# A convolution feeding a multiplicative FFN: the first group's last two rounds convolved by VectorE and GpSimd

## The chip, the cores and the metric

One Trainium2 chip, one of its cores. The metric is the device time of one execution in microseconds (us). The engines of the core: TensorE (PE in the profile; PEld its weight loads), VectorE (DVE), ScalarE (ACT), GpSimd (POOL) and SyncE (SP). SyncE, ScalarE and GpSimd issue DMA transfers, each on a queue of its own. Every engine works through its instructions in the order in which the program lists them.

## The reference

```python
# x (8, 3904, 192), weight (8 heads, 7 taps)
w = softmax(weight, axis=-1)
x_pad = concatenate([zeros((8, 6, 192)), x], axis=1)       # each sequence
out[b, s, h, g] = sum_k w[h, k] * x_pad[b, s + k, h * 24 + g]
x = out.reshape(31232, 192)
a = x @ w1                                                # (192, 1024)
b = x @ w2                                                # (192, 1024)
h = a * b @ w3                                            # (a * b) @ w3, (1024, 1024)
return h @ w_out                                          # (1024, 192)
```

A causal convolution with 7 taps over the tokens of each sequence, the same taps for the 24 channels of a head, and then a network in which two products are multiplied elementwise. The inputs are float32; the kernel computes in bfloat16 with float32 sums. It uses (a * b) @ (w3 @ w_out), so that W = w3 @ w_out (1024 x 192) is made once.

## The kernel before

**Rows and rounds.** The 31,232 tokens are cut into two halves ("rows" r = 0 and 1) of TS = 15,616, which run side by side: one on partitions 0 to 63, the other on 64 to 127, since 192 channels are three chunks of 64. A round is CH = 512 tokens of both halves; there are 31 (the last is half as long). Four rounds make a group. For each group the kernel runs the first products of its four rounds (`first_product`: for each of eight tiles of 128 columns, a and b by 12 matmuls at line 489, a cast of a by ScalarE at 497, the multiplication by VectorE at 508), and then its second products (`second_product`, line 540, one call per round and half, eight per group), whose results ScalarE copies to `osb` (545) and a DMA stores (552). `xT`, the convolved tokens with the channels on partitions, is a ring of four rounds.

**Where the convolved tokens come from.** There are three ways.

- *Blocks* (`SIZES`): windows of 64 tokens of which 58 come out (`ST`). TensorE multiplies a window by a banded matrix of taps (`conv`, line 398), ScalarE or VectorE evicts (419). Blocks 0 to 4 are transposed by TensorE straight into `xT` (rounds 0 to 3 and a bit more); from block 5 on they go to a DRAM buffer `rows` (`store`), and DMA transposes on SyncE's queue (`transposes`, 471) bring them into `xT`.
- *Separate blocks* (`ALONE`): 18 windows, 1,024 tokens, for the first two rounds of a half group; group p convolves them while its second products run, with `load_alone` (342) before and `store_alone` after.
- *Shared rounds* (`SHARED`): two rounds of 512 tokens, laid out with 128 stretches of tokens on partitions. GpSimd computes heads 0 to 3 with multiplications and additions (`shared_head`, lines 325 to 334) and VectorE heads 4 to 7 (317, 320; ScalarE starts each at 315). `load_shared` (279) brings the tokens, `pad_shared` (292) writes zeros over the six tokens ahead of a sequence's start, where a stretch begins with one; `store_shared` (364) writes `rows`. The tap k = 6 is taken first and reads nothing of those zeros; the taps k = 5 and lower read them.

Before the change, group 0 had no shared part: its second products had blocks 5, 6 and 7 between them (20, 20 and 14 windows), which made rounds 4 to 9. Shared and separate parts began with group 1 (rounds 10 and 11 shared, 12 and 13 separate).

**Order.** It is written out by hand: the program text gives the order on every engine, and a tile with several buffers makes an instruction wait for the last user of its buffer (`xb` has five, `xw` two: W3 transposed and the shared tokens; `convo` two). GpSimd in the beginning issues the loads of x and of the weights and copies weights; then `store(4, ...)` and W_out's load `wo_b` (664), `pace` (665: a two-element copy that makes GpSimd wait until W3's transposes are nearly done), and the loads of blocks 5, 6 and 7. SyncE transposes W3 (569). W = w3 @ w_out is made by `w3_product` (575) after round 3. The taps for the shared rounds are normalized in `wv` (lines 688 to 697) around that.

Of the kernel before, what the change touches and what calls it, by code (L numbers as in the profile page):

```python
# [16 lines left out]
def kernel(  # L17
# [30 lines left out]
    LAST = S - (WB - 1) * ST  # L48
# [9 lines left out]
    NB = len(SIZES)  # L58
# [3 lines left out]
    MAXN = SIZES[GRID - 1]  # L62

    def tok(i):
        return (i // WB) * S + (i % WB) * ST
# [40 lines left out]
    xb_of, zero_rows = {}, {}  # L106
# [5 lines left out]
    def load_x(b, parts=(0, 1)):  # L112
        tiles = xb_of.setdefault(b, [])
        zeros_of = zero_rows.setdefault(b, [])
        for i0, n in [v for e, v in enumerate(halves_of(b)) if e in parts]:
            xb = work.tile([128, n, D], BF16, tag="xb", bufs=5, name="xb")
            w = 0
            while w < n:
                i = i0 + w
                m = min(n - w, WB - i % WB)  # L120
                at_end = i + m == NWIN
                if at_end:
                    m -= 1
                if m:
                    for r in range(NS):
                        nc.gpsimd.dma_start(out=xb[Q * r:Q * r + Q, w:w + m, :],  # L126
                                            in_=x_spans(r, i, m))
                if i % WB == 0:
                    zeros_of += [(xb, 0, w), (xb, 1, w)]
                w += m  # L130
                if at_end:
                    nc.gpsimd.memset(xb[Q:128, w, :], 0.0)
                    t = tok(NWIN - 1) - PAD
                    nc.gpsimd.dma_start(out=xb[0:Q, w, :], in_=x_rows[t:t + Q, :])
                    nc.gpsimd.dma_start(out=xb[Q:Q + PAD + LAST, w, :],
                                        in_=x_rows[TS + t:TS + t + PAD + LAST, :])
                    w += 1
# [18 lines left out]
    diag = const.tile([128, Q + PAD], BF16)  # L156
    nc.vector.memset(zeros, 0.0)
# [45 lines left out]
    for i in range(2):  # L203
        copy_w(1, i, nc.gpsimd.tensor_copy)
    load_w(3)
# [130 lines left out]
    def load_alone(p):  # L336
        b, n = GRID - 1 + p, NA // 2
# [9 lines left out]
    def store_alone(p):  # L347
        convo, n = convo_of[GRID - 1 + p], NA // 2
# [75 lines left out]
    def store(b, first=0, last=NWIN, queue=nc.sync):  # L424
        n = SIZES[b] // 2
        last = min(last, FIRST[b] + 2 * n)
        stored[0] = tok(last) if last < NWIN else TS
        convo = convo_of[b]
        for c in range(2):
            i0 = FIRST[b] + c * n  # L430
            w, end = max(0, first - i0), min(n, last - i0)
            while w < end:
                left = WB - 1 - (i0 + w) % WB
                m = min(end - w, max(1, left))
                src = convo[Q * c:Q * c + ST, w:w + m].rearrange("s w k r g -> s w (k r g)")
                j0 = tok(i0 + w)
                if left == 0:
                    queue.dma_start(out=rows[j0:j0 + LAST, :], in_=src[0:LAST, 0, :])
                else:
                    dst = rows[j0:j0 + ST * m, :].rearrange("(w s) c -> s w c", s=ST)  # L440
                    for s0, s1 in ((0, 48), (48, ST)):
                        queue.dma_start(out=dst[s0:s1], in_=src[s0:s1])  # L442
# [196 lines left out]
    load_w3(CH)  # L639
    w3_transposes(0, range(JT))  # L640
# [4 lines left out]
    def send(last):  # L645
# [3 lines left out]

    first_product(0, {  # L650
        4: seq([(conv, 2, 0, 4)]),
# [12 lines left out]
    nc.gpsimd.dma_start(out=wo_b, in_=wor)  # L664
    P(out=pace, in_=w3T[0:1, JT - 3, DFF - 2:DFF])
# [8 lines left out]
    def zero(b):  # L674
        for xb, r, w in zero_rows.pop(b, []):
            nc.gpsimd.memset(xb[Q * r:Q * r + PAD, w, :], 0.0)
# [12 lines left out]
    nc.vector.tensor_tensor(  # L689
        out=wv, in0=wv, in1=top.unsqueeze(2).to_broadcast([128, H, K]), op=ALU.subtract)  # L690
    w3_product(0)
    nc.scalar.activation(out=wv, in_=wv, func=ACT.Exp)
    nc.vector.reduce_sum(out=top, in_=wv, axis=AX.X)
    nc.vector.reciprocal(out=top, in_=top)
    nc.vector.tensor_tensor(
        out=wv, in0=wv, in1=top.unsqueeze(2).to_broadcast([128, H, K]), op=ALU.mult)
    for jt in range(1, JT):
        w3_product(jt)
# [22 lines left out]
    for p, rounds in enumerate(groups):  # L721
# [3 lines left out]
        if p in SHARED:  # L725
# [6 lines left out]
            if p + 1 in SHARED:  # L732
                pad_shared(p + 1)
# [47 lines left out]
```

## Time and profile before

| | |
|---|---|
| median of 3 runs | 516.44 us (516.05 to 517.52) |
| profiled execution | 515.89 us, of which 514.2 are its span |
| TensorE busy | 508.4 us |
| VectorE busy | 401.1 us |
| ScalarE busy | 353.1 us |
| GpSimd busy | 321.4 us |

The profile is that of one execution. Its page gives each engine's busy time, the span in 40 slices, the DMA queues, the chain of waits that ended last, and the costliest groups of instructions by line; other views list the chain, or one engine's instructions, in order of time. In a row of the timeline stand the start, the length, the engine, the line, what it writes from what, the count, and in brackets the idle time ahead of it with what ended it. In a row of a group: the count, the least, median and greatest length in nanoseconds, the first and last start. `L489` is line 489 of the code. Rounds 0 to 3 run from about 9 to 59 us, W is made until 64.4, and group 0's second products end at 88.88.

### The profile page before, as it was taken

What the parts mean: (1) busy time and instruction counts of PE and PEld (TensorE: products, weight loads), DVE (VectorE), ACT (ScalarE), POOL (GpSimd) and SP (SyncE); (2) the same over time, 40 slices, a digit from 0 to 9 for tenths busy, and PEclk for the clock granted to TensorE, in tenths of its full rate; (3) what the DMA queues carried; (4) which work ended last, traced back from release to release, by engine and by line L of the source; (5) the groups of instructions that cost most, each with busy time, mean ns of one, the idle gap of its engine ahead of it and who ended that gap; (6) DMA issues with size and microseconds to landing.
All of it is one profiled execution on the core that took longest, in us unless ns stands there. A gap on an engine that the chain in (4) does not pass through costs nothing.

```text
span 514.2 us, 13632 instructions
## 1 busy us (share of the span) xinstructions
PE 508.4 (99%) x5608; PEld 339.1 (66%) x5608; DVE 401.1 (78%) x471; ACT 353.1 (69%) x469; POOL 321.4 (63%) x447
## 2 busy tenths in 40 slices
PE   8999999999999999999999999999999999999997
PEld 4555798454894458945598445985459845498587
DVE  6778723899959999499994999949999499972970
ACT  6887645777657776577765777657776577744762
POOL 8601534299999999699984999749997491000000
PEclk9999999999999999999999999999999999999999
DMA  8989999992965992787728787288842851035004
GB/s 118 155 152 127 134 216 231 207 197 54 193 193 149 137 108 94 237 146 102 95 93 248 141 104 91 93 255 134 93 51 94 259 112 32 2 102 171 6 3 155
DMA packets 137410, 67.91 MB, mean 132 GB/s; under 512 B 98899, under 2 KB 135939, under 8 KB 137283
## 3 DMA queue, kind: packets, MB, share of 16 engines
q0 software_dynamic: 48096, 26.92, 36.4%
q1 hardware_dynamic: 89105, 40.01, 32.7%
q8 instruction: 44, 0.72, 0.6%
q14 instruction: 19, 0.16, 0.1%
q10 hardware_dynamic: 146, 0.10, 0.1%
HBM read 39.60 MB, written 36.56 MB: 148 GB/s over the span
## 4 chain that ended last, share of the span: by engine, by line
PE 96%; DVE 2%; ACT 1%; issue 0%; ACTq 0%; DVEq 0%
PE pairs L489 60%; PE pairs L540 32%; PE pairs L398 2%; DVE abT L508 1%; PE pairs L575 1%; ACT asb L497 1%; PE pairs L451 1%; PE pairs L213 1%; DVE cprod L254 0%; ACT convo L419 0%; DVE convo L584 0%; ACT xT L463 0%; PE pairs L263 0%; PE pairs L615 0%; ACT osb L545 0%
## 5 line engine op out<-in xcount | busy, mean ns | idle before, releaser
L508 DVE TENSOR_TENSOR abT<-asb,pairs 128x1024 bf16<-128x1024 bf16 (+1 forms) x245 | 298.2, 1217 | 69.5 <-ACT asb L497 53.0
L489 PE MATMUL pairs<-xT,wd 64*128 64x512 bf16 (+2 forms) x3000 | 319.8, 371 | 0.7 <-DVE abT L508 0.3
L497 ACT CAST asb<-pairs 128x1024 bf16<-128x1024 f32 (+1 forms) x245 | 247.1, 1009 | 67.7 <-PE pairs L489 67.4
L489 PEld LDWEIGHTS <-wd 64*128 64x128 bf16 x3000 | 160.7, 94 | 153.6 <-issue 1.5
L540 PE MATMUL pairs<-W_sb,abT 128*128 128x192 bf16 x1952 | 165.0, 246 | 0.0
L540 PEld LDWEIGHTS <-abT 128*128 128x128 bf16 x1952 | 159.9, 98 | 5.3 <-issue 5.1
L545 ACT COPY osb<-pairs 128x384 f32<-128x384 f32 x122 | 58.6, 480 | 83.4 <-PE pairs L540 82.6
L331 POOL TENSOR_TENSOR acc<-acc,term 128x384 f32<-128x384 f32 (+1 forms) x120 | 107.3, 894 | 9.4
L328 POOL TENSOR_TENSOR term<-xv,wv 128x384 f32<-128x384 bf16 (+1 forms) x144 | 107.7, 748 | 0.5 <-DMA xv<-zeros 0.5
L317 DVE SCALAR_TENSOR_TENSOR pairs<-xv,wv,pairs 128x384 f32<-128x384 bf16 (+1 forms) x120 | 68.7, 572 | 7.2 <-ACT pairs L315 3.4
L364 POOL DMA_DIRECT2D rows<-y x6 | 3.7, 614 | 70.2 <-DVE y L320 61.3
L334 POOL TENSOR_TENSOR y<-acc,term 128x192 bf16<-128x192 f32 (+5 forms) x60 | 26.5, 467 | 1.9
L419 ACT CAST convo<-pairs 128x864 bf16<-128x864 f32 (+9 forms) x49 | 26.5, 613 | 0.2
L325 POOL TENSOR_TENSOR acc<-xv,wv 128x384 f32<-128x384 bf16 (+1 forms) x24 | 18.3, 764 | 9.7 <-DMA xv<-in_x_dram 9.6
L419 DVE CAST convo<-pairs 128x960 bf16<-128x960 f32 (+4 forms) x10 | 8.2, 858 | 17.2 <-PE pairs L398 17.2
L320 DVE SCALAR_TENSOR_TENSOR y<-xv,wv,pairs 128x192 bf16<-128x192 bf16 (+5 forms) x60 | 18.0, 351 | 1.1
L126 POOL DMA_DIRECT2D xb<-in_x_dram x20 | 13.9, 715 | 4.1 <-DMA xb<-in_x_dram 2.3
L342 POOL DMA_DIRECT2D xb<-in_x_dram x20 | 15.1, 772 | 0.0
L552 POOL DMA_DIRECT2D out_dram<-osb x8 | 6.1, 763 | 12.3 <-ACT osb L545 9.3
L279 POOL DMA_DIRECT2D xv<-in_x_dram x12 | 13.0, 1087 | 0.0
L315 ACT ACTIVATE pairs<-xv,wv 128x384 f32<-128x384 bf16 (+1 forms) x24 | 12.8, 550 | 0.0
L442 POOL DMA_DIRECT2D rows<-convo x2 | 1.1, 544 | 18.1 <-ACT convo L419 18.1
(65 smaller groups left out, 86.9 us busy)
## 6 DMA issues: line engine op xcount, KB each, us to landing
out_dram<-osb SPq DMA_DIRECT2D x52, 384.0 KB
xv<-in_x_dram POOLq DMA_DIRECT2D x10, 672.0 KB, 9.7
xb<-in_x_dram POOLq DMA_DIRECT2D x20, 216.0 KB, 7.3
rows<-y POOLq DMA_DIRECT2D x5, 768.0 KB, 5.9
out_dram<-osb POOLq DMA_DIRECT2D x8, 384.0 KB, 5.2
w3rows<-in_moe_w_dram POOLq DMA_DIRECT2D x2, 1024.0 KB, 11.8
xb<-in_x_dram POOLq DMA_DIRECT2D x8, 240.0 KB, 8.0
rows<-convo SPq DMA_DIRECT2D x6, 288.0 KB
```

The source lines that it names most:

```text
L317: f.scalar_tensor_tensor(out=flat, in0=xs(k), scalar=tap(k), in1=flat, op0=ALU.mult, op1=ALU.add)
L320: f.scalar_tensor_tensor(out=dst, in0=xv[:, 0:W, r, h * G + cs.start:h * G + cs.stop], scalar=tap(0), in1=by_row[:, :, r, cs], op0=ALU.mul ...
L325: f.tensor_tensor(out=flat, in0=xs(PAD), in1=wide(PAD), op=ALU.mult)
L328: f.tensor_tensor(out=term.rearrange("p (m g) -> p m g", g=G), in0=xs(k), in1=wide(k), op=ALU.mult)
L331: f.tensor_tensor(out=acc, in0=acc, in1=term, op=ALU.add)
L334: f.tensor_tensor(out=dst, in0=by_row[:, :, r, cs], in1=term[:, :, r, cs], op=ALU.add)
L419: f[e % len(f)](out=dst, in_=part)
L489: nc.tensor.matmul(p[:, r, e * n:e * n + n], wd[i][rs, k, ft * 128:(ft + 1) * 128], xT[k][rs, r0 + c0:r0 + c1], start=(k == 0), stop=(k == ...
L497: nc.scalar.copy(out=asb, in_=pa)
L508: nc.vector.tensor_tensor(out=dst, in0=asb, in1=pb, op=ALU.mult)
L540: nc.tensor.matmul(ops[:, (g - g0) * D:(g - g0) * D + D], ab[:, jt, r, g * 128:(g + 1) * 128], W_sb[:, jt, :], start=(jt == 0), stop=(jt = ...
L545: f(out=osb[:, g0:g0 + per, :].rearrange("p g d -> p (g d)"), in_=ops[:, 0:per * D])
```

## The change

Block 5 has 18 windows and is the last of the ordinary blocks. Rounds 6 and 7 become the shared part of group 0, rounds 8 and 9 its separate block. The shared part is loaded in round 0, after the second half of W3. GpSimd computes its first four heads between W_out's load and the end of the group; the loads of block 5, of the separate block and of the next shared part stand between these heads on its queue, and `pace` stands behind head 0. VectorE's four heads go between the second products, and one pair of PSUM banks is held for them, as in later groups. The taps' load moves from SyncE's queue, behind W3's transposes, to GpSimd's at the start, and their softmax moves from the W products to round 0: maximum and subtraction behind the tile ft = 2, the exponential and the rest behind ft = 3. The stores of group 0's outputs move from GpSimd's queue to ScalarE's. `load_x` and `store` lose the cases that no block needs any more.

```diff
-    SIZES = [6, 4, 8, 10, 8, 20, 20, 14]
-    SHARED = {p: ((p + 2) * GROUP - 2, min((p + 2) * GROUP, NR)) for p in range(1, 7)}
-    ALONE = {p: (p + 2) * GROUP for p in range(1, 6)}
+    SIZES = [6, 4, 8, 10, 8, 18]
+    SHARED = {p: ((p + 2) * GROUP - 2, min((p + 2) * GROUP, NR)) for p in range(7)}
+    ALONE = {p: (p + 2) * GROUP for p in range(6)}
...
-    MAXN = SIZES[GRID - 1]
+    MAXN = 10
...
         copy_w(1, i, nc.gpsimd.tensor_copy)
+    nc.gpsimd.dma_start(out=wv, in_=bass.AP(
+        tensor=weight.tensor, offset=0, ap=[[0, 128], [K, H], [1, K]]))
     load_w(3)
...
     load_x(4)
     load_w3(CH)
+    load_shared(0)
     w3_transposes(0, range(JT))
...
+    def taps_max():
+        nc.vector.reduce_max(out=top, in_=wv, axis=AX.X)
+        nc.vector.tensor_tensor(
+            out=wv, in0=wv, in1=top.unsqueeze(2).to_broadcast([128, H, K]), op=ALU.subtract)
+
+    def taps_exp():
+        nc.scalar.activation(out=wv, in_=wv, func=ACT.Exp)
+
+    def taps_scale():
+        nc.vector.reduce_sum(out=top, in_=wv, axis=AX.X)
+        nc.vector.reciprocal(out=top, in_=top)
+        nc.vector.tensor_tensor(
+            out=wv, in0=wv, in1=top.unsqueeze(2).to_broadcast([128, H, K]), op=ALU.mult)
+
     first_product(0, {
+        2: taps_max,
+        3: seq([(taps_exp,), (taps_scale,)]),
         4: seq([(conv, 2, 0, 4)]),
...
     store(4, need(GROUP - 1) - 1, queue=nc.gpsimd)
     nc.gpsimd.dma_start(out=wo_b, in_=wor)
+    pad_shared(0)
+    shared_head(0, 0, nc.gpsimd)
     P(out=pace, in_=w3T[0:1, JT - 3, DFF - 2:DFF])
     load_x(5)
-    load_x(6)
-    wv = const.tile([128, H, K], FP32)
-    top = const.tile([128, H], FP32)
-    nc.sync.dma_start(out=wv, in_=bass.AP(
-        tensor=weight.tensor, offset=0, ap=[[0, 128], [K, H], [1, K]]))
+    shared_head(0, 1, nc.gpsimd)
+    load_alone(0)
+    shared_head(0, 2, nc.gpsimd)
+    load_shared(1)
+    shared_head(0, 3, nc.gpsimd)
     first_product(3)
...
-    load_x(7)
-    zero(6)
-    nc.vector.reduce_max(out=top, in_=wv, axis=AX.X)
...
-    SHORT, LONG = range(0, 6), range(6, H)
     at = {
-        (0, 0): [(conv_heads, 5, SHORT, (V, A))],
-        (0, 1): [(conv_heads, 5, LONG), (put_rows, 5, 2 * GROUP - 1)],
-        (0, 4): [(conv_heads, 6, SHORT, (V, A))],
-        (0, 5): [(conv_heads, 6, LONG), (put_rows, 6, 2 * GROUP - 1)],
-        (0, 6): [(load_shared, 1), (conv_heads, 7, range(H), (A, V), 3)],
-        (0, 7): [(put_rows, 7, 2 * GROUP - 1)]}
-    for p in ALONE:
-        at[p, 0] = [(conv_heads, GRID - 1 + p, range(0, 4), (A,))]
-        at[p, 3] = [(conv_heads, GRID - 1 + p, range(4, H), (A,)), (store_alone, p)]
+        (0, 0): [(conv_heads, 5, range(0, 4), (A,))],
+        (0, 1): [(conv_heads, 5, range(4, H), (A,)), (put_rows, 5, GROUP + 1)],
+        (0, 4): [(conv_heads, GRID, range(0, 4), (A,))],
+        (0, 6): [(conv_heads, GRID, range(4, H), (A,)), (store_alone, 0)]}
+    for p in range(1, len(ALONE)):
+        at[p, 0] = [(conv_heads, GRID + p, range(0, 4), (A,))]
+        at[p, 3] = [(conv_heads, GRID + p, range(4, H), (A,)), (store_alone, p)]
...
-            for h in range(0, 4):
+            for h in range(0, 4 if p else 0):
...
-            second_product(R, r, R == NR - 1 and r == 1, nc.sync if p else nc.gpsimd)
+            second_product(R, r, R == NR - 1 and r == 1, nc.sync if p else nc.scalar)
```

More of the change, by code (lines that the diff above doesn't have):

```diff
@@ L61 @@
     EARLY = SIZES[0] * ST
-    MAXN = SIZES[GRID - 1]
+    MAXN = 10
+    assert sum(SIZES[:GRID]) * ST >= SHARED[0][0] * CH and sum(SIZES[:GRID]) < WB
     def tok(i):
@@ L105 @@
     x_rows = x.rearrange("b s d -> (b s) d")
-    xb_of, zero_rows = {}, {}
+    xb_of = {}
     def x_spans(r, i, m):
@@ L110, in x_spans, with load_x @@
                        ap=[[D, Q], [ST * D, m], [1, D]])
-    def load_x(b, parts=(0, 1)):
+    def load_x(b):
         tiles = xb_of.setdefault(b, [])
-        zeros_of = zero_rows.setdefault(b, [])
-        for i0, n in [v for e, v in enumerate(halves_of(b)) if e in parts]:
+        for i0, n in halves_of(b):
             xb = work.tile([128, n, D], BF16, tag="xb", bufs=5, name="xb")
[L117 to L137, printed above, removed]
+            for r in range(NS):
+                nc.gpsimd.dma_start(out=xb[Q * r:Q * r + Q], in_=x_spans(r, i0, n))
             if len(halves_of(b)) == 1:
@@ L156 @@
     diag = const.tile([128, Q + PAD], BF16)
+    wv = const.tile([128, H, K], FP32)
+    top = const.tile([128, H], FP32)
     nc.vector.memset(zeros, 0.0)
@@ L432, in store @@
             while w < end:
-                left = WB - 1 - (i0 + w) % WB
-                m = min(end - w, max(1, left))
+                m = end - w
                 src = convo[Q * c:Q * c + ST, w:w + m].rearrange("s w k r g -> s w (k r g)")
                 j0 = tok(i0 + w)
[L437 to L442, printed above, removed]
+                dst = rows[j0:j0 + ST * m, :].rearrange("(w s) c -> s w c", s=ST)
+                for s0, s1 in ((0, 48), (48, ST)):
+                    queue.dma_start(out=dst[s0:s1], in_=src[s0:s1])
                 w += m
@@ L684, in put_rows @@
         send(last)
-    load_x(7)
-    zero(6)
-    nc.vector.reduce_max(out=top, in_=wv, axis=AX.X)
[L689 to L697, printed above, removed]
+    for jt in range(JT):
         w3_product(jt)
```

13 lines of the change are left out of this document (4 added, 9 removed).

## The prediction

> **What bounds the kernel now.** I read the busy times and the chain of waits first, then the chain in order of time (start, length, what), then GpSimd's timeline, since most of the edit lands on GpSimd's queue, and last how long that queue's transfers take to land.
>
> ```profile
> span 514.2 us, 13632 instructions
> PE 508.4 (99%) x5608; PEld 339.1 (66%) x5608; DVE 401.1 (78%) x471; ACT 353.1 (69%) x469; POOL 321.4 (63%) x447
> PE 96%; DVE 2%; ACT 1%; issue 0%; ACTq 0%; DVEq 0%
> ```
>
> ```profile
> 15.86 1.23 DVE abT L508
> ...
> 17.13 1.47 PE pairs L489 x12
> 18.60 0.29 PE pairs L398 x16
> ...
> 59.00 5.39 PE pairs L575 x64
> 64.39 2.64 PE pairs L540 x32
> 67.03 0.74 PE pairs L398 x24
> ...
> 70.51 0.33 PE pairs L398 x8
> ...
> 78.87 0.74 PE pairs L398 x24
> ...
> 82.36 0.33 PE pairs L398 x8
> ...
> 85.43 0.70 PE pairs L398 x32
> ...
> 88.88 41.55 PE pairs L489 x384
> 130.43 2.75 PE pairs L540 x32
> 133.17 0.49 PE pairs L398 x16
> 133.67 8.03 PE pairs L540 x96
> 141.69 0.49 PE pairs L398 x16
> 142.19 10.67 PE pairs L540 x128
> ```
>
> TensorE is the path: from 43 us to the end each piece of the chain starts where the last one ended. So a microsecond of TensorE work taken out is a microsecond gained, and a microsecond in which TensorE waits is one lost; no later idle time takes it back. Only in round 0 do VectorE and ScalarE stand on the path (15.86: a product on VectorE frees the bank pair that TensorE takes at 17.13). From 64.39 to 88.88 us are group 0's second products; rounds 4 to 7 follow in 41.55 us, 10.39 each, so round 6 starts at 88.88 + 20.78 = 109.66 us.
>
> **TensorE work saved.** Blocks 5, 6 and 7 cost 0.74 + 0.33 + 0.74 + 0.33 + 0.70 = 2.84 us of convolution (L398). Now 18 windows remain as block 5 and 18 come in as a new separate block, each the size of the separate block in group 1, 0.49 + 0.49. Group 1's stretch of second products is 142.19 + 10.67 − 130.43 = 22.43 us with one such block, and with two 23.41; before it was 88.88 − 64.39 = 24.49. Saving: 1.08 us, group 0's products then ending at 87.80.
>
> **The softmax of the taps inside round 0.**
>
> ```profile
> 59.00:63.00 4.00, 1.05 (x5) 1.00 1.57 188
> ...
> 61.06 0.25 ACT L692 ACTIVATE wv<-wv 128x56 f32<-128x56 f32 x1 [0.94 <-DVE wv L689]
> ...
> 12.93 1.24 POOL L176 DMA_DIRECT2D wd<-in_moe_w_dram  x2
> ```
>
> The first row is the five small VectorE instructions (1.05 us in 59 to 63 us, where they cost nothing, as TensorE waits there for none of them). Moved behind the multiplications of tiles 2 and 3 they stand in front of the product at 15.86. The maximum and subtraction (0.42) delay that product, and with it the first-product matmuls at 17.13; the exponential (0.25) and the other three (0.63) delay the next product, whose bank the convolution at 18.60 takes. By then VectorE is late by about 1.05 us less the 0.1 of slack, so I take 0.95 us. Below, 0.4 (only the first two bite). Above: the load of the taps is now issued by GpSimd at 12.93, and if it lands later than 15.85 VectorE waits, up to about 1 us more, 2.0 in all. The issue itself pushes GpSimd's next copies by about 0.6 us (1.24 for two issues); that falls inside the same delay.
>
> **GpSimd's new work and what queues behind it.** Before, GpSimd idled until the row at 52.78, then only issued transfers until 103. Columns: start, length, engine, line, what.
>
> ```profile
> 39.19 1.07 POOL L442 DMA_DIRECT2D rows<-convo  x2 [18.09 <-ACT convo L419]
> 40.25 0.96 POOL L664 DMA_DIRECT2D wo_b<-in_moe_w_out_dram  x1
> 52.78 0.17 POOL L665 COPY pace<-w3T 1x2 bf16<-1x2 bf16 x1 [11.57 <-DMA w3T<-w3rows]
> 53.31 5.48 POOL L126 DMA_DIRECT2D xb<-in_x_dram  x8 [0.36 <-PE pairs L489]
> ...
> 102.99 0.83 POOL L325 TENSOR_TENSOR acc<-xv,wv 128x384 f32<-128x384 bf16 x1 [9.56 <-DMA xv<-in_x_dram]
> ...
> 115.06 0.83 POOL L325 TENSOR_TENSOR acc<-xv,wv 128x384 f32<-128x384 bf16 x1
> ...
> 127.10 2.24 POOL L279 DMA_DIRECT2D xv<-in_x_dram  x2
> 129.34 0.86 POOL L325 TENSOR_TENSOR acc<-xv,wv 128x384 f32<-128x384 bf16 x1
> ...
> 141.73 0.82 POOL L325 TENSOR_TENSOR acc<-xv,wv 128x384 f32<-128x384 bf16 x1
> ```
>
> One head takes 115.06 − 102.99 = 12.07 us, 127.10 − 115.06 = 12.04 for the second, 141.73 − 129.34 = 12.39 for the third (it crosses a chunk). The tile is as large in group 0 (1,024 tokens, 128x384), so four heads are 48.5 us, all on an engine that works in order, with the loads of block 5, of the separate block and of the next shared tile between them. These landing times (least, median, most) set the rest: the load of W_out; the zeros over a sequence's start; a separate block's four loads, first issue at 167.57 and the fourth landing last; the store of y:
>
> ```profile
> DMA to landing us min/median/max: 8.3/8.3/8.3
> ```
> ```profile
> DMA to landing us min/median/max: 2.5/3.6/4.7
> ```
> ```profile
> 167.57 3.04 POOL L342 DMA_DIRECT2D xb<-in_x_dram  x4
> ```
> ```profile
> DMA to landing us min/median/max: 4.2/6.3/8.6
> ```
> ```profile
> DMA to landing us min/median/max: 3.5/5.1/6.7
> ```
> ```profile
> 50.03 1.26 SPq L569 DMA_TRANSPOSE w3T<-w3rows  x1
> ```
>
> Rounds 6 and 7 (tokens 3072 to 4095) contain the sequence start at 3904, so head 0 needs those zeros from its second instruction on. *When is that?* The store of block 4 waits for ScalarE at 39.19, which the 0.95 shifts to 40.14; W_out's load is issued from 41.2, the zeros behind it at 42.2. If the zeros overtake, they land 2.5 us later, 44.7. If GpSimd's queue lands in order, they come with W_out: 41.2 + 8.3 = 49.5. The four loads above landed one after another in the order of issue, so I take 49.0, near that end; with the new shared load ahead of both it could be 51.5.
>
> The Trainium skill speaks here too, in "DMA: Bandwidth & Descriptors", SWDGE vs HWDGE vs iDMA: GpSimd's DMAs have only one queue. That would put the zeros behind W_out, as taken. The same page's fit in Anatomy of one DMA (2.0 us plus bytes over 436 GB/s) would land W_out's 384 KB after 2.9 us, where the row has 8.3; by the fit, an estimate, the zeros would come at about 44.7 and round 6 would be some 4 us less late; the measurement decides.
>
> From 49.0: rest of head 0 (12.07 − 0.83) 60.2; pace copy 60.4 (the transposed W3 it waits for was there at 52.78, and may be 7 us later unnoticed); four loads of block 5 at 5.48/8 each, 2.7, 63.1; head 1, 75.2; four loads of the separate block, 3.0, 78.2; head 2, 90.6; the next shared load, 2.2, 92.8 (its buffer, W3's, is free since the W products); head 3, 104.9; the store of y lands 5.1 later, 110.0; three transposes on SyncE: the third is issued 2 × 1.3 later and lands 2.75 after its issue, as that of 50.03 let the copy at 52.78 go: **115.3 us, where round 6 started at 109.66.**
>
> **What TensorE meets on the way.** Four loads need at most 10.8 us from first issue to last landing (169.85 + 8.6 − 167.57). These share the engines with transposes; where the queue is alone it moves about 190 GB/s (the GB/s in the first row above), so 0.88 MB take 4.7 and, with some 2.5 to start and finish, 7.2 at least. Block 5: 60.4 + 7.2 to 10.8 = 67.6 to 71.2, wanted at 67.03 + 0.95 = 67.98. Separate block: 75.2 + 7.2 to 10.8 = 82.4 to 86.0, wanted after the fifth product, 64.39 + 11.26 + 0.49 + 2.67 = 78.8 (79.8 with the 0.95). So TensorE waits at one or both convolutions and the products end 3.6 to 7.2 late against 87.80, at 91.4 to 95.0; round 6 could start at 112.2 to 115.8. It starts when both are there: 115.3 to 115.8, and I take 115.4. **Sum: 115.4 − 109.66 = +5.7 us** on the profiled execution's 515.89, that is 521.6; the median of the runs shown is 516.44, so the same sum on it would be 522.1. The 0.95 and the 1.08 are inside that sum, not beside it.
>
> **What costs nothing.** VectorE's heads 4 to 7 run in group 0's products, where it evicted the old blocks, as in group 1; it is done some 20 us before GpSimd. Output stores on ScalarE's queue: one issue there took
>
> ```profile
> L548 ACTq DMA_DIRECT2D out_dram<-osb x1: 383/383/383, 511.3 to 511.3; - x1
> ```
>
> 0.38 us, eight are 3.1 us in a stage of 23.4 us whose 16 output copies (0.48 each) leave the engine over half idle; uncovered it would be 3.1 us. Group 1 is not touched: GpSimd enters it 5 us late, but so does TensorE.
>
> **Rivals.**
> *Not slower: GpSimd's queue gets through in time.* Mechanism: the zeros overtake W_out (44.7) and transfers are quick (3.5 for y, 7.2 for a load). Then round 6's rows are there at 109.4 and the separate block at 78.1, before it is wanted. Left are 0.95 − 1.08 = −0.1 us: 515.8, or 515.2 with 0.4 for the softmax. It decides when the zeros land before about 45 us. For it: the row of 2.5 us; against it: W_out's 8.3. 19%.
> *The W3 transposes starve.* The shared load, two transfers of the size in the first row below (9.7 us to land), comes into the stretch of W3's transposes, the second row.
>
> ```profile
> xv<-in_x_dram POOLq DMA_DIRECT2D x10, 672.0 KB, 9.7
> ```
> ```profile
> L569 SPq DMA_TRANSPOSE w3T<-w3rows x16: 1182/1259/5157, 27.6 to 52.6; - x16
> ```
>
> The longest of them, 5.2 us, is already one that stands behind GpSimd's loads, as I read it. If all but the first are put off by another 8.2 us, the last lands at 52.6 + 8.2 + 2.75 = 63.6, where the fifth W product wants it at 59.00 + 0.95 + 2.70 = 62.65, and the pace copy is released at 61.0 instead of 60.4: +1 us on the sum, 522.6. Against it: some 7 us of slack. 10%.
> *The clock falls while TensorE waits.* Here it would be a wait of over 3 us at the separate block and another at round 6, each followed by a stretch of slower matmuls; if 3.4 us after each ran at half speed, 1.7 us each, 523.3 to 525.0. The granted clock is 1.00 in the window row above, but no gap of that length lies there. 6%. The Trainium skill, "TensorE: Matmul & The Clock Gate", Part 1: The HAM clock gate, states it: an idle window of about 3.4 us halves the clock. No run here shows it yet.
>
> **How the numbers follow.** The forecast as worked out (GpSimd's chain late, 517.5 to 526) has 62%; the three rivals 35%; 3% is for a gain that I can't name. The range: downwards it takes in the upper end of the first rival, since with 44.7 for the zeros even slow loads (10.8) make the stretch only some 1.8 us longer; upwards, 51.5 for the zeros, 6.7 for y and 0.6 from the pace copy make +10.4, 526.3. Range 515.6 to 526.5; the forecast's own 517.5 to 526. A measurement of this kernel can tell about 0.3%, 1.5 us. The most that TensorE can gain is 1.08, under that: faster 0.04, same 0.20, slower 0.76.
>
> **What would show it.** In the changed kernel's profile: head 0's second GpSimd instruction waiting for zeros till 49; the load of the separate block issued near 75; TensorE gaps before the first convolution of that block and before round 6, its matmuls waiting for a DMA, together 5 to 7 us; L398's pieces in group 0 adding up to 1.96; softmax pieces on the chain near 16 to 18 us. I am wrong if GpSimd's fourth head in group 0 ends before 99 us, or if group 0 and rounds 4 to 7 show no gap on TensorE.

## The result, and the profile after

The change made the kernel slower, in the direction of the forecast and, by the medians, by four times its size.

| | before | after |
|---|---|---|
| median of six runs, us | 516.70 | 539.18 |
| lowest and highest, us | 516.05, 517.52 | 532.67, 540.70 |
| ratio, 95% interval | | 1.0394 [1.0331, 1.0456] |
| profiled execution, time / span, us | 515.89 / 514.2 | 532.67 / 531.0 |

The profiled execution is the fastest of the six: +16.8 us in it have to be found place by place, and the six runs' spread needs a reason as well. The ratios, here and below, are formed from means and leave out executions more than 1.5% above the fastest of their kernel (540.70 here, 546.18 and 547.50 in experiment 2). First the page of the kernel after: span, busy times, and the engines' shares of the chain of waits.

```profile
span 531.0 us, 13643 instructions
PE 511.4 (96%) x5576; PEld 341.8 (64%) x5576; DVE 408.4 (77%) x491; ACT 358.4 (67%) x478; POOL 363.7 (68%) x496
PE 82%; DMA 10%; POOL 6%; issue 0%; ACT 0%; POOLq 0%; ACTq 0%
```

Span less busy time of TensorE was 514.2 − 508.4 = 5.8 us and is 19.6 now; transfers hold 10% of a chain on which they had no share worth a place before. Its pieces in order of time (start, length, what):

```profile
22.08 25.65 DMA xv<-in_x_dram
...
48.32 5.94 DMA xv<-zeros
...
68.00 9.24 DMA xb<-in_x_dram
77.28 0.88 PE pairs L381 x10
78.16 4.47 PE pairs L519 x32
83.12 8.03 PE pairs L519 x96
...
96.66 7.43 DMA xT<-rows
104.14 17.06 PE pairs L468 x157
121.20 4.94 DMA xT<-rows
126.18 20.46 PE pairs L468 x188
146.65 2.75 PE pairs L519 x32
```

The chain enters through the load of the shared tile (25.65 us), goes on through the zeros, GpSimd's head 0 and block 5's load, and reaches TensorE at 77.28. Round 6, which started at 109.66, starts at 126.18, 16.5 us later. Group 1's second products start at 146.65 instead of 130.43, and from there to the end the two kernels differ by 0.6 us: nearly all of the loss has arisen by round 6. GpSimd's timeline (start, length, line, what, in brackets the idle time before and what ended it):

```profile
20.98 2.21 POOL L262 DMA_DIRECT2D xv<-in_x_dram  x2
...
48.32 0.55 POOL L275 DMA_DIRECT2D xv<-zeros  x1 [5.65 <-DMA xv<-in_x_dram]
...
54.32 0.83 POOL L311 TENSOR_TENSOR term<-xv,wv 128x384 f32<-128x384 bf16 x1 [4.56 <-DMA xv<-zeros]
...
65.73 3.04 POOL L116 DMA_DIRECT2D xb<-in_x_dram  x4
...
80.83 2.99 POOL L325 DMA_DIRECT2D xb<-in_x_dram  x4
...
96.37 2.25 POOL L262 DMA_DIRECT2D xv<-in_x_dram  x2
...
111.06 0.62 POOL L347 DMA_DIRECT2D rows<-y  x1 [0.30 <-POOL y L317]
```

The order is the forecast's; its first line is not. The zeros, which overwrite a part of the shared tile, wait until that tile has landed at 47.7 and are issued only at 48.32. Everything behind them is 5 us late. TensorE's waits in that stretch:

```profile
69.60 0.25 PE L381 MATMUL pairs<-xb,Aband 64*64 64x216 bf16 x1 [1.14 <-DMA xb<-in_x_dram]
70.79 0.25 PE L381 MATMUL pairs<-xb,Aband 64*64 64x216 bf16 x1 [0.94 <-DMA xb<-in_x_dram]
75.68 0.34 PE L381 MATMUL pairs<-xb,Aband 64*64 64x216 bf16 x1 [4.64 <-DMA xb<-in_x_dram]
77.28 0.88 PE L381 MATMUL pairs<-xb,Aband 64*64 64x216 bf16 x13 [1.26 <-DMA xb<-in_x_dram]
...
101.66 0.39 PE L468 MATMUL pairs<-xT,wd 64*128 64x512 bf16 x2 [1.07 <-DMA xT<-rows]
```

TensorE stands for 1.14 + 0.94 + 4.64 + 1.26 = 8.0 us in front of block 5, and the 32 products behind it take 4.47 us, where as many take 2.75 at 146.65. The windows (stretch, length, busy time and count of PE, PEld, DVE, ACT, POOL, then granted clock, DMA share, GB/s) say why:

```profile
72.00:75.00 3.00, 0.00 (x0) 0.00 (x0) 2.81 (x7) 0.00 (x0) 2.84 (x4) 0.50 1.13 201
75.00:78.00 3.00, 1.05 (x14) 0.61 (x13) 0.00 (x0) 0.16 (x1) 2.84 (x5) 0.50 0.14 25
78.00:81.00 3.00, 3.00 (x23) 2.77 (x20) 0.00 (x0) 1.69 (x4) 2.92 (x5) 0.50 0.03 5
```

The clock is halved through all three. Windows of one microsecond show where that begins and ends:

```profile
71.00:72.00 1.00, 0.04 (x1) 0.00 (x0) 0.93 (x3) 0.00 (x0) 1.00 (x2) 0.72 1.09 104
...
81.00:82.00 1.00, 1.00 (x10) 0.97 (x9) 0.00 (x0) 0.35 (x1) 1.00 (x2) 0.66 0.00 0
```

A mean of 0.72 puts the fall at about 71.4 us, while TensorE waits, and 0.66 puts the return at about 81.7. That also bears on the spread of the six runs: 532.67 us had a mean clock of 0.990, 534.04 one of 0.987, and 539.18 to 540.7 had 0.981 to 0.983. An estimate from these means: the clock accounts for at most some 4 to 5 of the 6.5 us between the profiled execution and the median, and for less where TensorE was waiting anyway. A second profile of the same kernel (experiment 8) has another half-clock stretch, below.

Last, why a load whose transfers landed 9.7 us after their issue in the kernel before (the median of ten; group 1's needed up to 14.8) took 25.65. First it stood behind another transfer of its own queue. In the windows 29 to 30, 30 to 31 and 32 to 33 us GpSimd's queue (q0) carried (packets, MB, share of the 16 engines):

```profile
q0 software_dynamic: 13, 0.43, 197.6%
...
q0 software_dynamic: 3, 0.10, 45.6%
...
q0 software_dynamic: 197, 0.07, 69.1%
```

Up to 31 us these are a few large packets, of about 33 KB: the second half of W3, issued at 20.46. The small packets of the shared tile run only from about 32 us, so that some 10 of the 25.65 us went by before this load moved anything. Then it shared the engines: while it and W_out's load are in flight, the queues of GpSimd and SyncE (q1, here the transposes of W3) carried, in the windows 42 to 45 and then 45 to 48 us:

```profile
q0 software_dynamic: 851, 0.33, 86.9%
q1 hardware_dynamic: 854, 0.21, 54.3%
...
q0 software_dynamic: 884, 0.35, 86.9%
q1 hardware_dynamic: 884, 0.21, 53.7%
```

One packet of the one, one packet of the other. GpSimd's queue moves 0.33 to 0.35 MB in 3 us, 110 to 117 GB/s, where the window row quoted in the forecast had 188 GB/s. At 33 to 36 us it was 0.27 MB (715 packets against 710). An estimate: alone, at 188 GB/s, the load's 1.38 MB would have moved in some 7.3 us; from 32 to 47.7 it took 15.7. The Trainium skill, "DMA: Bandwidth & Descriptors", Queues, rings and completion order, states that a DMA engine takes turns among the queues that have work for it, packet by packet; the equal counts agree.

### The profile page after: what moved, and what is told of

Its sections match the earlier page's. It is cut to its first block, busy times and chain, and to the rows that moved or that the text cites. A ratio compares the mean times of both kernels' runs of the same rounds, so it can differ in the third digit from the quotient of the medians.

```text
span 531.0 us, 13643 instructions
## 1 busy us (share of the span) xinstructions
PE 511.4 (96%) x5576; PEld 341.8 (64%) x5576; DVE 408.4 (77%) x491; ACT 358.4 (67%) x478; POOL 363.7 (68%) x496
## 4 chain that ended last, share of the span: by engine, by line
PE 82%; DMA 10%; POOL 6%; issue 0%; ACT 0%; POOLq 0%; ACTq 0%
PE pairs L468 51%; PE pairs L519 30%; DMA xv<-in_x_dram 5%; DMA xT<-rows 2%; DMA xb<-in_x_dram 2%; POOL xb L116 1%; PE pairs L381 1%; DMA xv<-zeros 1%; POOL acc L314 1%; POOL term L311 1%; POOL wd L178 1%; POOL wd L157 1%; POOL xb L160 0%; POOL y L317 0%; POOL xb L170 0%
## 5 line engine op out<-in xcount | busy, mean ns | idle before, releaser
L468 PE MATMUL pairs<-xT,wd 64*128 64x512 bf16 (+3 forms) x3000 | 320.6, 371 | 5.2 <-DMA xT<-rows 3.8
L314 POOL TENSOR_TENSOR acc<-acc,term 128x384 f32<-128x384 f32 (+1 forms) x140 | 127.4, 910 | 11.0
L311 POOL TENSOR_TENSOR term<-xv,wv 128x384 f32<-128x384 bf16 (+1 forms) x168 | 127.8, 761 | 5.3 <-DMA xv<-zeros 5.3
L300 DVE SCALAR_TENSOR_TENSOR pairs<-xv,wv,pairs 128x384 f32<-128x384 bf16 (+1 forms) x140 | 81.1, 579 | 23.5 <-ACT pairs L298 19.0
L347 POOL DMA_DIRECT2D rows<-y x7 | 4.3, 613 | 72.9 <-issue 47.7
L402 ACT CAST convo<-pairs 128x864 bf16<-128x864 f32 (+6 forms) x54 | 29.7, 622 | 11.2 <-PE pairs L381 10.6
L317 POOL TENSOR_TENSOR y<-acc,term 128x192 bf16<-128x192 f32 (+5 forms) x70 | 31.4, 474 | 2.2
L308 POOL TENSOR_TENSOR acc<-xv,wv 128x384 f32<-128x384 bf16 (+1 forms) x28 | 21.7, 776 | 2.3 <-DMA xv<-in_x_dram 2.1
L381 PE MATMUL pairs<-xb,Aband 64*64 64x216 bf16 (+4 forms) x384 | 12.5, 241 | 8.9 <-DMA xb<-in_x_dram 8.0
L325 POOL DMA_DIRECT2D xb<-in_x_dram x24 | 18.0, 770 | 0.0
L381 PEld LDWEIGHTS <-Aband 64*64 64x64 bf16 x384 | 7.6, 107 | 14.3 <-issue 14.0
## 6 DMA issues: line engine op xcount, KB each, us to landing
xv<-in_x_dram POOLq DMA_DIRECT2D x12, 672.0 KB, 10.2
```

Of the source, the lines that this page charges most:

```text
L300: f.scalar_tensor_tensor(out=flat, in0=xs(k), scalar=tap(k), in1=flat, op0=ALU.mult, op1=ALU.add)
L308: f.tensor_tensor(out=flat, in0=xs(PAD), in1=wide(PAD), op=ALU.mult)
L311: f.tensor_tensor(out=term.rearrange("p (m g) -> p m g", g=G), in0=xs(k), in1=wide(k), op=ALU.mult)
L314: f.tensor_tensor(out=acc, in0=acc, in1=term, op=ALU.add)
L317: f.tensor_tensor(out=dst, in0=by_row[:, :, r, cs], in1=term[:, :, r, cs], op=ALU.add)
L381: nc.tensor.matmul(view(slice(Q * c, Q * c + Q), r)[:, :, j * G:(j + 1) * G], band_of(h, r), xb[Q * r:Q * r + Q, w0:w0 + n, h * G:(h + 1) ...
```

## The experiments

Theory A: one chain on GpSimd's queue sets group 0, as forecast, and it is long because transfers meet the transposes. Theory B: one part of the edit (block 5's place, the softmax, the presence of the shared load) carries most of the loss and the rest is hidden. Times are medians, ratios are to the kernel before on the same chip.

**1. Block 5's and the separate block's loads ahead of head 0** (kernel after).

```
     pad_shared(0)
+    load_x(5)
+    load_alone(0)
     shared_head(0, 0, nc.gpsimd)
     P(out=pace, in_=w3T[0:1, JT - 3, DFF - 2:DFF])
-    load_x(5)
     shared_head(0, 1, nc.gpsimd)
-    load_alone(0)
```

> The changed kernel with the loads of block 5 and of the separate block issued by GpSimd ahead of head 0 instead of behind heads 0 and 1. Theory A (one chain on GpSimd sets the time: shared load, zeros, four heads, store of y, transposes, round 6): TensorE's gap before block 5 (9.2 us) and most of that before round 4 (7.4) vanish, but round 6 starts only 5 to 7 us sooner than its 126.1 us, because head 3 ends at about 105.5 instead of 110.8; the time stays far above the kernel before, 525 to 531 us. Rival B (each gap costs on its own): what is left is the gap before round 6, 4.9 us, so 517 to 521 us.

528.11 us, 1.0215 [1.0196, 1.0234]. A's time held, B's fell. TensorE's longest wait is now one, and it is at round 6:

```profile
65.52 2.24 PE L554 MATMUL pairs<-wo_b,w3T 128*128 128x192 bf16 x25 [1.37 <-DMA w3T<-w3rows]
...
118.02 12.19 PE L468 MATMUL pairs<-xT,wd 64*128 64x512 bf16 x90 [5.79 <-DMA xT<-rows]
```

The two moves return 11 us of the median, but they uncover round 6, because the four heads and y's store, issued at 107.0 instead of 111.06, are only 4 us earlier; and the moved loads now hold up W3's transposes, for which the W products wait 1.37 us. The places are links of one chain, not separate prices.

**2. The shared load one step earlier** (kernel after; `load_shared(0)` ahead of `load_w3(CH)`).

```
+    load_shared(0)
     load_w3(CH)
-    load_shared(0)
```

> The changed kernel with the shared load issued ahead of the second half of W3 instead of behind it. Theory A (the shared load lands at 47.7 us because its packets alternate with those of W3's transposes): it lands at 38 to 42 us, the zeros at 46 to 50 instead of 54.3, head 3 ends 4 to 8 us sooner and the time falls by as much, to 526 to 531 us where the clock stays; the transposes of W3 end later, by less than 6 us, and TensorE does not wait for them. Rival (the shared load is slow by itself, 25 us wherever it stands): it still needs some 25 us, lands at 46 us, and the time moves by less than 2 us.

542.74 us, 1.0399 [1.0362, 1.0436], where the kernel after has 1.0394: no gain, and A's number fell. The load still took up to 26.8 us to land, though W3's second half no longer stood ahead of it; W3's transposes begin at 27 us either way, so it meets them all the same. Nearly all of its packets had moved by 38 us; why its last transfer landed only at 48.3 stays open. The rival's time came out, but experiment 6 speaks against a load that is slow wherever it stands.

**3. TensorE kept busy in the waits** (kernel after; unused matmuls, as many as fill each wait).

```
+        (0, 0): [(warm, 34), (conv_heads, 5, range(0, 4), (A,))],
...
+            if p == 1 and j in (0, 2):
+                warm(18 if j else 28)
```

> The changed kernel with 34, 28 and 18 matmuls of zeros (7.3, 6.0 and 3.9 us at full clock) put into TensorE's three gaps: ahead of block 5, of round 4 and of round 6. Their results are not used. Theory C (the clock falls in the gaps, and that makes both the spread of 532.7 to 540.7 us and 1.7 us of the profiled run): granted clock 1.00, second products behind block 5 back at 2.75 us from 4.47, spread under 2 us, median 529 to 533. Rival (the spread comes from the transfers): spread and median as before, 539, with the clock at 1.00.

544.62 us (543.83 to 545.18), mean clock 0.994, 1.0536 [1.0516, 1.0555]. The filled wait did what C said of it: the 32 products behind it took 2.81 us at a clock of 1.00 (4.54 in the same row of the kernel after). For the time the run is inconclusive: the wait moved on to the separate block (3.57 us, with the clock at 0.50 at 96 to 99 us), and the fillers at rounds 4 and 6, some 6 and 4 us long, came where no gap was left and cost their length. The spread of its runs is 1.35 us against the 8.0 of the kernel after, which fits a spread that comes from the clock but doesn't show it.

**4. The softmax alone** (kernel before; taps loaded by GpSimd at the start).

```
+        2: taps_max,
+        3: seq([(taps_exp,), (taps_scale,)]),
         4: seq([(conv, 2, 0, 4)]),
```

> The kernel before with one part of the change alone: the load of the taps issued by GpSimd at the start and their softmax inside round 0. The prediction's term is 0.95 us (0.4 to 2.0). From the changed kernel's trace, where the matmuls behind that place start 1.1 us later and W's product 1.5 us later, I expect 1.1 to 1.5 us, ratio 1.002 to 1.003; rival: the delay is taken back by the waits of rounds 1 and 2, under 0.4 us, ratio below 1.001.

518.88 us over twelve runs, 1.0047 [1.0028, 1.0067]: +2.4 us, by the interval 1.4 to 3.5, where 1.1 to 1.5 was expected and the term's upper end was 2.0. VectorE's row for the subtraction (L656), TensorE's next product, and VectorE's row for the last multiplication (L665):

```profile
17.46 0.99 DVE L656 TENSOR_TENSOR wv<-wv,top 128x56 f32<-128x56 f32 x1
...
19.64 1.47 PE L493 MATMUL pairs<-xT,wd 64*128 64x512 bf16 x12 [1.16 <-DVE abT L512]
...
19.98 0.22 DVE L665 TENSOR_TENSOR wv<-wv,top 128x56 f32<-128x56 f32 x1
```

Both instructions took 0.22 us in their old places. Here GpSimd copies weights from 17.51 to 19.1, beside the subtraction and not beside the multiplication. In the kernel after, its copies run to 15.6 and again from 17.52 to 19.1, and it is the multiplication (L641) that is slow, not the subtraction (L632):

```profile
15.92 0.22 DVE L632 TENSOR_TENSOR wv<-wv,top 128x56 f32<-128x56 f32 x1
...
17.66 0.80 DVE L641 TENSOR_TENSOR wv<-wv,top 128x56 f32<-128x56 f32 x1
```

**5. Only the shared load, in the kernel before** (a spare tile of the same size, at the same place on GpSimd's queue, filled from x).

```
+    spare = work.tile([128, 8 + PAD, NS, D], BF16, tag="xw", bufs=2, name="spare")
+    for r in range(NS):
+        nc.gpsimd.dma_start(out=spare[:, :, r, :], in_=bass.AP(...))
```

> The kernel before with the shared load alone added where the change puts it (behind the second half of W3), into a tile that nobody reads. Theory A (packets of GpSimd's queue and of SyncE's transposes take turns): the 1.3 MB land only after 22 to 27 us, where the same load takes 6 to 15 in the rest of the kernel, and W3's transposes end 2 to 4 us later, at 55 to 57 us, unnoticed by TensorE; time as before within 1 us. Rival (the changed kernel's other work makes the load slow): it lands after 9 to 15 us, as elsewhere.

A single run, 519.7 us against 516.23 before. It landed 20.6, 23.3 and 26.1 us after issue (least, median, most), as A had it; so the load is slow without anything else of the change. W3's transposes now last from 25.95 to 56.9 us and pace is released at 56.56 instead of 52.78: both sides pay. The time was to stay within 1 us and didn't; of the 3.5, some 1.8 are a stretch of half clock at 9 to 12 us, ahead of the added load, and 1.42 a wait for transposed rows at 113.79.

**6. The shared load ahead of all of W3** (kernel after; W3's first half thereby also moves behind the copies and the load of x).

```
-    load_w3(0)
     for i in range(2):
         copy_w(3, i, P)
+    load_shared(0)
     load_x(4)
+    load_w3(0)
     load_w3(CH)
-    load_shared(0)
```

> The changed kernel with the shared load ahead of both halves of W3, so that it runs before the transposes begin. Theory A: it lands within 12 us, by 32 us; then the zeros wait only for GpSimd's turn and for the load of W_out: they land at 47 to 51 us instead of 54.3, the whole chain of GpSimd is 3 to 7 us sooner, and the time falls to 524 to 534 us. W3's transposes start 6 us later and end by 60 us, just in time. Rival (after moving the load ahead of the second half only, which gained nothing: the load is slow wherever it stands): it needs over 20 us again and the time does not fall.

536.32 us, 1.0378 [1.0354, 1.0403]. The shared load landed in 7.6, 9.3 and 11.0 us: ahead of W3 and away from the transposes it is as quick as the median of the kernel before, so the load is not slow by itself. This run takes away both the place behind W3 and the meeting with the transposes; how much each of them cost is read from the packets above, and no run separates them. The time, which was to be 524 to 534, was missed. Now W3's transposes start at 37.5 and end at 62.9, and the separate block's loads, issued at 77.23, run beside block 5's store, the output stores on ScalarE's queue (q10) and, from 83.23, the transposes of rounds 4 and 5: at 85 to 88 us 571, 358 and 387 packets of GpSimd's, ScalarE's and SyncE's queue. TensorE waits 13.0 us for them, of which two waits:

```profile
90.86 0.39 PE L381 MATMUL pairs<-xb,Aband 64*64 64x216 bf16 x1 [4.12 <-DMA xb<-in_x_dram]
94.97 0.34 PE L381 MATMUL pairs<-xb,Aband 64*64 64x216 bf16 x1 [3.72 <-DMA xb<-in_x_dram]
```

**7. All remedies at once** (shared and W_out loads first; later places for the separate block; next shared load behind y's store; three heads on GpSimd and five on VectorE; softmax by a matmul that broadcasts the row).

```
+    load_shared(0)
     load_x(4)
+    load_w3(0)
     load_w3(CH)
-    load_shared(0)
+    nc.gpsimd.dma_start(out=wo_b, in_=wor)
...
-    shared_head(0, 0, nc.gpsimd)
+    shared_head(0, 1, nc.gpsimd)
     P(out=pace, in_=w3T[0:1, JT - 3, DFF - 2:DFF])
     load_x(5)
-    shared_head(0, 1, nc.gpsimd)
+    shared_head(0, 2, nc.gpsimd)
...
+        (0, 6): [(conv_heads, GRID, range(0, 4), (A,))],
+        (0, 5): [(shared_head, 0, 0, nc.vector)]}
```

> A version made from the readings so far: shared load and W_out ahead of W3 and the transposes, block 5 convolved one and the separate block two products later, the next shared load behind the store of y, GpSimd with three heads in group 0 and VectorE with five, and the taps' softmax taken from the first one by a matmul that spreads it over the partitions (taps rounded to bfloat16 for the shared rounds too) instead of a load and five instructions in round 0. Theory A: no gap on TensorE behind 43 us, so what is left is the 1.08 us of convolution saved: 514.8 to 516.0, ratio 0.997 to 0.999. Rival (something else in the change costs, such as output stores on ScalarE's queue or VectorE's heads in group 0): 517 us or more with no GpSimd chain in the waits.

527.91 us, 1.0209 [1.0175, 1.0242]; 514.8 to 516 was missed, for the reason of experiment 6: the separate block's loads, issued at 76.0, meet the same three, and TensorE waits 0.80 + 4.78 + 2.61 us.

**8. The kernel after, once more**, unchanged.

> The changed kernel itself once more, for a profile of one of its longer executions. Theory C (the clock halves after gaps, by chance of when a gap begins): in an execution of about 539 us the granted clock is 0.5 not only behind the gap before block 5 but also behind a later one, 18 to 20 us in all. Rival: same clock stretches as in the profile at hand, and the longer time stands in transfers.

536.83 us, mean clock 0.987. It has the half clock at 72 to 81 us again, and another where the first profile has none (columns as in the windows above):

```profile
129.00:132.00 3.00, 3.00 (x19) 1.30 (x17) 1.22 (x1) 1.61 (x2) 2.92 (x5) 0.56 0.52 118
```

In this second profile TensorE also waits at 90 to 93 us, before the separate block. Adding up the windows, its clock is halved for 13.6 us instead of 10.2, not for 18 to 20. The additional 3.4 us cost some 1.7 of the 4.2 us between the two executions; the rest stands in waits. So executions of one binary differ in which transfer arrives late and in how often the clock then falls.

**9, 10. Another order, with the shared load left where it is** (block 5 loaded during the wait for the zeros; separate block and next shared tile together behind pace; convolutions of the separate block at products 7 and 8; softmax by matmul; experiment 9 has three GpSimd heads, experiment 10 four).

```
     pad_shared(0)
     load_x(5)
     shared_head(0, 1, nc.gpsimd)
     P(out=pace, in_=w3T[0:1, JT - 3, DFF - 2:DFF])
     load_alone(0)
     load_shared(1)
     shared_head(0, 2, nc.gpsimd)
     shared_head(0, 3, nc.gpsimd)
```

> A second version from the readings: the shared load stays behind W3; GpSimd loads block 5 while it waits for the zeros, then one head, then the separate block and the next shared part together, before the transposes of rounds 4 and 5 begin, then two heads; VectorE takes five heads; the separate block is convolved behind products 7 and 8; the separate block of group 1 is loaded behind GpSimd's first head of that group; taps for the shared rounds from the first softmax by a matmul, rounded to bfloat16. Theory A (what costs is transfers that meet transposes, and the chain on GpSimd behind them): the store of y is issued near 94 us, round 6 finds its rows, no wait of TensorE above 1.5 us behind 43 us; 515.0 to 517.5 us. Rival (any such order leaves some transfer late): one gap of over 3 us remains, 519 us or more.

> The same order with GpSimd's four heads and VectorE's four, as in the change. Theory A: the store of y is issued 12 us later, near 106 us, and round 6, due at 109 to 110, waits until about 117 to 120: 7 to 10 us more than with three heads, 523 to 528. Rival (the number of heads is not what counts, only the transfers): within 2 us of the version with three heads.

525.51 us, 1.0183 [1.0156, 1.0209], and 525.34, 1.0185 [1.0157, 1.0213]: the number of heads on GpSimd makes no difference there, and both expected times were missed. With four heads y's store was issued at 107.14 instead of 95.57, but round 4 started so late that round 6 found its rows all the same. In experiment 9 the convolutions no longer wait, but round 4 does:

```profile
90.91 0.39 PE L471 MATMUL pairs<-xT,wd 64*128 64x512 bf16 x2 [2.08 <-DMA xT<-rows]
95.33 0.61 PE L471 MATMUL pairs<-xT,wd 64*128 64x512 bf16 x2 [4.04 <-DMA xT<-rows]
```

**11, 12. The next shared load behind y's store**, in the kernel after and in experiment 9's.

```
-    load_shared(1)
...
+            load_shared(1)
```

> The changed kernel with one move: the next shared load goes from between heads 2 and 3 to behind the store of y. Theory A (that load takes turns with the transposes of rounds 4 and 5): round 4's transposes land within 5 us of their issue instead of 7 to 9, TensorE's gap before round 4 (3.1 us) shrinks below 1 us, the store of y is issued 2.2 us sooner; the time falls by 1 to 4 us against the changed kernel. Rival (round 4 is late only because block 5 was): gap unchanged, and the time with it.

> The version with three heads once more, with one move: the next shared load goes behind the store of y, so that from 75 us no load of GpSimd's queue meets block 5's store and the transposes of rounds 4 and 5. Theory A: the store lands within 5 us instead of 7, round 4's transposes land before round 4 is due at about 88 us, no gap over 1.5 us is left on TensorE behind 43 us, 515 to 518 us. Rival (the transposes are slow because of the output stores on ScalarE's queue or of the separate block's load, not of that load): a gap of 3 us or more before round 4 stays, 521 us or more.

In the kernel after: 534.86 us, 1.0341 [1.0307, 1.0375], 4.3 us under its median; the waits before round 4 are gone, and those before block 5, the separate block (1.48) and round 6 (2.17) stay. y's store landed in 3.6 us there instead of 7.6. In experiment 9's order: 519.25 us, 1.0052 [1.0039, 1.0065], 6.3 us under experiment 9, mean clock 0.999 to 1.0, all six runs within 0.9 us. What was expected, 515 to 518, was missed by a little, and the rival (521 or more) fell. The chain in order of time:

```profile
92.75 9.32 PE pairs L471 x85
102.07 9.92 DMA xT<-rows
112.03 20.46 PE pairs L471 x188
132.50 2.75 PE pairs L522 x32
```

Round 6 at 112.03 is 2.4 us later than before, and that is nearly the whole loss; its transposes, from 99.38, run beside the next shared load, issued at 94.16. With the work divided nearly as in the kernel after, 20 of its 22.5 us are regained by order and places, by the softmax as a matmul (experiment 4 has some 2 us for it) and by the head moved to VectorE; no run separates these. The output stores on ScalarE's queue were not tried alone either: experiment 12 has them too and loses 2.7 us in all. None of the twelve beats the kernel before.

## Why the prediction was right or wrong

**What was right.** The chain itself: zeros, four heads with loads between them, y's store, transposes. From 54.32 to 110.76, where head 3 ends, it took 56.4 us, where the forecast had 55.9 (49.0 to 104.9). The zeros landed behind W_out, as taken, and did not overtake it: 52.5 and 54.3 us here, 48.2 and 48.4 in experiment 6, 45.6 and 47.3 in experiment 7. TensorE waits at block 5, at round 4 (which was not foreseen) and at round 6, but in this profile not at the separate block, where a gap was named as a sign (in experiment 8 there is one, of 2.25 us); GpSimd's fourth head ends well after the 99 us that would have refuted it. TensorE's saving came out: behind block 5's first piece come only three more convolution pieces, of 0.49 us each as in group 1. W3's transposes, the rival with 10%, did not starve: their last packets moved before 58 us, and the W products did not wait for them.

**The first step that failed: "From 49.0".** It asked whether the zeros overtake W_out, and did not ask whether the shared tile had landed; that load was taken to be there long before. Behind W3's second half until about 32 us, and then packet by packet in turn with the transposes, it landed at 47.7; the zeros, issued only then, landed at 54.3: +5.3 us. The bound of 51.5 was too low as well. Experiments 5 and 6 show it: 20.6 to 26.1 us when the load stands behind W3 and meets its transposes, 7.6 to 11.0 ahead of both. And where it is there in time, in experiment 6, head 0 goes on within 0.6 us of the forecast's 49.0:

```profile
48.47 0.83 POOL L311 TENSOR_TENSOR term<-xv,wv 128x384 f32<-128x384 bf16 x1 [4.28 <-DMA xv<-zeros]
```

Having seen SyncE's transposes start between 27.6 and 52.6 us, I priced what they would suffer from the load, but not what the load would suffer from them, nor that W3, which they wait for, stands ahead of the load on its own queue.

**The terms at the other end were mis-sized for the same reason.** y's store took 7.6 us to land, not 5.1 (+2.5), since the next shared load, issued at 96.37, was still on GpSimd's queue (3.6 us with that load moved behind it, experiment 11); the load's landing times (least, median, most):

```profile
DMA to landing us min/median/max: 13.0/16.1/19.1
```

The last of it lands near 116.6 (the second issue, about 97.5, and 19.1), the store at 118.7. The three transposes took 126.18 − 118.67 = 7.5, not 5.35 (+2.1), beside the loads of group 1's separate block, issued at 111.67. With the heads' 0.5 and 0.3 us before the store, the chain's error is 5.3 + 0.5 + 0.3 + 2.5 + 2.1 = 10.7, which is 126.1 − 115.4 for round 6.

**"What TensorE meets on the way" was too short.** Block 5's loads were issued at 65.73 instead of 60.4 and needed 11.5 us, a little above the bound of 10.8; no transpose was under way, and why they needed it I can't say (from 72 to 75 us an output store on ScalarE's queue moved 467 packets beside their 682). With the clock, the late convolution and the softmax, TensorE's own path, which was to reach the end of group 0's products at 87.80 if nothing waited, reached it at 100.2: 1.3 for the start, 8.0 of waiting, 1.2 for convolution pieces that run singly, 1.7 for products at half clock. Then come 3.2 us at the start of round 4 (1.07 and 2.09), whose rows are late: block 5's rows are stored only from 85.35, beside the separate block's loads (126 packets against 608 at 88 to 90 us), and their transposes, at 92.61 to 104.0, run beside the output stores on ScalarE's queue (350 against 561 at 92 to 94 us) and in the end beside the next shared load; rounds 4 and 5 stood nowhere in the sum. So without GpSimd's end of the chain TensorE would have come to round 6 at 104.14 + 20.46 = 124.6, only 1.6 us sooner. That is why removing one link (experiments 1, 6, 11) returned at most 11 us: another lay just behind it. The forecast took the later of two paths, rightly, but had the same transfer times wrong on both.

**The clock rival had the mechanism, not its weight.** It was given 6% and 1.7 us per wait, a size that the profile bears out (4.47 against 2.75 us). What I missed is that waits of that length were likely as soon as the chain was 5 us later, and that further ones come and go between executions: the median is 6.5 us above the profiled execution. The Trainium skill, "TensorE: Matmul & The Clock Gate", Part 1, has an idle window of about 3.4 us halve the clock. These traces agree only in part. Here the clock fell at about 71.4, 0.4 us into the wait of 4.64 us, and 3.0 us after the products ended at 68.45, with two matmuls of 0.25 us in between. The stretch from 100.6 to 104.14, with 0.39 us of matmuls in it, left the clock at 1.00. In experiment 8 a wait of 2.61 us, up to 127.78, was followed by half clock from about 129.3. The length of a single wait did not decide it.

**The softmax** was 0.95 us with a bound of 2.0; alone it costs 2.4 (experiment 4; 1.4 to 3.5 by the interval). The instruction counts and the place were right; the durations came from a stretch in which GpSimd copied nothing. In the kernel after, the W products start at 60.4 instead of 59.0, a delay that the wait for block 5's load covers.

## What to carry to other kernels

When a transfer moves into a stretch where another queue already works, take its landing time from rows where both queues are busy, and price what each does to the other; a landing time from a quiet stretch is a lower bound only. On an in-order queue the first late transfer moves everything behind it, so ask of the first link whether its own input has landed, and what stands ahead of that input on its queue. Where two paths meet, price both to the end: removing the later one gains only up to the next.

## What the runs showed of the hardware beyond that

- Packets of the two queues alternate one for one (715 to 710, 851 to 854, 884 to 884 in 3 us), although those of GpSimd's loads carry more (0.35 against 0.21 MB). Three queues shared the engines in the same way at 106 to 108 us: 368, 365 and 366 packets of GpSimd's, ScalarE's and SyncE's queue in 2 us. The same 1.38 MB load took up to 25.65 us behind W3's second half and beside W3's transposes, and at most 11.0 ahead of both.
- A VectorE instruction with two inputs (a subtraction or multiplication of 128x56 elements) took 0.22 us with no GpSimd copy beside it, 0.80 and 0.99 with one.
- Half clock also came at about 8 to 13 us in the profiles of experiments 4 and 5, though 5 differs from the kernel before only from 20 us on; what starts it there stays open.
